# The first MoE's slices taken in halves: two pairs of batches in turn, with their sums in two parts through DRAM

## The chip, the cores and the metric

The kernel runs on one core of a Trainium2 chip. The core has a matrix engine (TensorE, PE in the profile), VectorE (DVE), ScalarE (ACT), GpSimd (POOL), and SyncE (SP), whose queue issues nearly all transfers between DRAM and the on-chip memory. Each engine runs its instructions in the order in which the program has them; between engines, semaphores order the work. The metric is the device time of one execution in microseconds (us).

## The reference, cut to what matters

Three layers stand one behind the other. Batches are 8, heads 8, positions 576, head width 64; `x` has 8 x 576 = 4608 rows of 512.

```python
p_packed = sm_attn(p, k, v)                 # 32 packed rows per head attend to 576 keys
out = sm_attn(q, p_packed, p_packed)        # 576 rows per head attend to the 32 packed rows
x = out.transpose(0, 2, 1, 3).reshape(4608, 512)
h = max(max(x @ w1, x @ w2), x @ w3)        # first MoE: 512 -> 768
x2 = h @ w_out                              # 768 -> 512
h = x2 @ w_in2                              # second MoE: 512 -> 2048, then a ratio of polynomials g(h)
return g(h) @ w_out2
```

The weights arrive as 64-bit floats. TensorE multiplies in a reduced 32-bit form, so each operand is split into a high and a low part and each product takes three matmuls.

## The kernel before

**Stages.** The work up to `x2` goes by four pairs of batches, `bp` = 0 to 3; the second MoE follows in blocks of 512 rows and is not touched. Instead of forming `x`, the kernel multiplies the softmax of the second attention (`a2`) with `m`, the product of the packed values and the weights (`m_stage`, two for each slice). `h` has 768 columns, in six slices `f` of 128. For a pair, the loop over `f` and the two batches calls `y_stage`; each has three steps `w`, one for each of `w1`, `w2`, `w3`: 12 matmuls into a `psy` bank, then a copy to `hm` on ACT (`w` = 0) or a maximum into `hm` on DVE (`L451`). Such a step is called a turn here: 36 make the y part of a pair. Behind it eight `x2_stage`s (two batches, four column blocks `m`) sum all six slices with `w_out`, 36 matmuls each; the sum is copied to a tile `hm` by ACT, for `m` = 3 by DVE (`L467`), and stored to `x2_scr` in DRAM.

**What runs between the turns.** After each turn the function `between` calls an `m_stage` for the next slice, one step of a script (`PACK` in the y part, `SECOND` in the x2 part) with the attention of the next pair, and, at some turns, `feed.step()`. The script's letters: `L`, `W`, `l` load keys, values and queries; `S`, `T`, `V`, `Z` are the first attention of one of four units; `s`, `g` the second attention.

**Weights.** A `feed.step()` finishes one piece of weights and starts the next. `decode` turns a piece of 64-bit floats into two parts: `L75`, `L76`, `L88`, `L90` on DVE, `L77` and others on ACT, `L85` and `L95` on POOL. The 30 pieces of the first MoE (24 of `w123`, four per slice, 384 columns; 6 of `w_out`, 512 columns) come before and during pair 0, one at every turn from its start until they are used up. A `w123` piece goes into a tile `wt`, is used by pair 0 from there and stored to `w_scr`; pairs 1 to 3 load it again (72 loads). The 32 pieces of the second MoE (512 columns) are fed during pairs 1 to 3, through the same four `wt` buffers, and stored to DRAM.

**Order.** The order of instructions on each engine is not the order of the code alone: a list scheduler with a timeline of its own places each instruction once its inputs are ready there, so work of a later `feed.step()` can stand ahead of its turn. On the chip that order is fixed.

Of the kernel before, what the change touches and what calls it, by code (L numbers as in the profile page):

```python
# [33 lines left out]
def attn_moe_moe2_kernel(  # L34
# [206 lines left out]
    NKT, NPT = 4, 3  # L241
# [11 lines left out]
    def s2_stage(u, qt, done):  # L253
# [25 lines left out]
        ah = a2p.tile([128, S], F32R, name=f"a2h{g}{b2}")  # L279
        al = a2p.tile([128, S], F32R, name=f"a2l{g}{b2}")  # L280
# [154 lines left out]
    hp_pool = bstack.enter_context(tc.tile_pool(name="hp_pool", bufs=1))  # L435

    def y_stage(b2, f, m, a2, between):
# [15 lines left out]
        hh = hp_pool.tile([128, S], F32R, name=f"hh{b2}{f}")  # L453
        hl = hp_pool.tile([128, S], F32R, name=f"hl{b2}{f}")
# [37 lines left out]
    for f in range(1, 6):  # L492
        pieces += [w_piece(f, hp) for hp in HPS] + wo[f + 2 : f + 3]
# [16 lines left out]
    feed2 = None  # L510

    y_steps = {1: range(1, 36, 4), 2: range(1, 36, 4), 3: range(1, 32, 4)}
    windows = (), (0, 2, 4, 6), (1, 3, 5)
    for bp in range(NBP):
        turn = itertools.count()
        if bp == 1:
            feed2 = Feed(wp, w2_pieces(), bufs=NRAW)
        a2, mt = ahead.a2, ahead.mt
        hs = [[None] * 6, [None] * 6]
        if bp + 1 < NBP:  # L520
            ahead = Ahead(bp + 1)
            for x in "L0 W0 L1 W1".split():
                ahead.do(x)
            pack = ahead.steps(PACK)
        else:
            pack = iter(())
        for f in range(6):
            if f < 5:
                nmt = m_tiles(f + 1)

            def between(bp=bp, f=f):
                t = next(turn)
                if f < 5 and t % 6 in (1, 3):
                    m_stage(bp, t % 6 // 2, nmt)
                if t >= 2:
                    next(pack, None)
                if bp == 0:
                    feed.step()
                elif t in y_steps[bp]:
                    feed2.step()  # L540
# [3 lines left out]
            for b2 in range(2):  # L544
                hs[b2][f] = y_stage(b2, f, mt[b2], a2[b2], between)
            mt = nmt
        if bp + 1 < NBP:
            assert not list(pack)
            gen = ahead.steps(SECOND)
            if bp == 0:  # L550
                assert not feed.raw and not feed.half
            for b2 in range(2):
                for m in range(4):
                    x2_stage(2 * bp + b2, m, hs[b2])
                    next(gen, None)
                    if 4 * b2 + m in windows[bp]:
                        feed2.step()
            next(gen, None)
            assert not ahead.soft
        else:  # L560
            assert not feed2.raw and not feed2.half
# [21 lines left out]
            for b2 in range(2):  # L583
                for m in range(4):
# [135 lines left out]
```

## Time and profile before

| what | value |
|---|---|
| median of 3 runs | 1429.55 us (1428.72 to 1430.9) |
| the profiled execution's own time | 1429.64 us |
| its span, first to last instruction | 1427.9 us (1.7 us lie around it) |
| busy: PE, DVE, ACT, POOL | 1337.6, 1093.5, 893.0, 351.1 us |
| mean granted TensorE clock | 0.973 of full speed |
| first matmul of the second MoE | about 630 us |

The change touches what lies before about 630 us. Busy shares over the whole span are means over stages with different limits, so the stages have to be read one by one; the rows of a stretch give the busy time of each engine in it, the granted clock (1.00 is 2.4 GHz, 0.50 is 1.2 GHz) and the load of the DMA engines.

### The profile page before, as it was taken

To read this page: it belongs to the slowest core of one execution; us is meant where nothing else is said; L and a number is where in the kernel's file an instruction comes from. 1 tells how busy PE (TensorE), PEld (TensorE's weight loads), DVE (VectorE), ACT (ScalarE), POOL (GpSimd) and SP (SyncE) were. 2 spreads that over 40 slices of the span, in tenths; PEclk is the share of its full clock that TensorE was granted. 3 is DMA by queue.
4 is the path that set the end of the run, shared out by engine and by line. 5 is a ranking of instruction groups with operands and counts; after the bars stand their busy time and mean duration, and the time that the engine had idled before them with its cause. 6 is when DMAs were issued, how large, how long until landed. Compare 5 with 4: busy or idle time off the path is not lost.

```text
span 1427.9 us, 21290 instructions
## 1 busy us (share of the span) xinstructions
PE 1337.6 (94%) x8016; PEld 1140.2 (80%) x8016; DVE 1093.5 (77%) x1712; ACT 893.0 (63%) x1523; POOL 351.1 (25%) x350
## 2 busy tenths in 40 slices
PE   5468899998999899999999999999999999999998
PEld 2257799887988799998888888888888888888886
DVE  5999854668475848339897888978888888888887
ACT  4577743655355536337686766868677686676765
POOL 4676632447444555300010100101001010000000
PEclk9598999999999999999999999999999999999999
DMA  9757662768556645583010100101001010010000
GB/s 290 224 188 220 221 232 78 245 209 297 173 174 228 240 165 192 180 293 154 1 59 1 56 4 7 53 1 60 1 8 52 1 52 1 11 42 0 31 1 30
DMA packets 76743, 159.72 MB, mean 112 GB/s; under 512 B 11104, under 2 KB 35680, under 8 KB 75872
## 3 DMA queue, kind: packets, MB, share of 16 engines
q1 hardware_dynamic: 76352, 157.84, 33.0%
q8 instruction: 63, 1.03, 0.3%
q10 hardware_dynamic: 288, 0.52, 0.1%
q14 instruction: 40, 0.33, 0.1%
HBM read 113.25 MB, written 45.09 MB: 111 GB/s over the span
## 4 chain that ended last, share of the span: by engine, by line
PE 76%; DMA 7%; DVE 3%; ACT 2%; issue 1%; SPq 0%; POOL 0%; DVEq 0%; ACTq 0%; POOLq 0%
PE po L61 9%; PE po L63 9%; PE po L62 9%; PE psh L62 9%; PE psh L61 9%; PE psh L63 9%; PE psy L61 6%; PE psy L63 6%; PE psy L62 6%; DMA w_raw<-in_w_dram 3%; DMA wi_b<-w_scr 2%; DMA w_scr<-wt 1%; DVE wt L88 1%; PE pst L363 1%; DVE ml L58 1%
## 5 line engine op out<-in xcount | busy, mean ns | idle before, releaser
L619 ACT ACTIVATE hb<-psh,babs 128x512 f32<-128x512 f32 (+1 forms) x145 | 100.1, 690 | 190.0 <-PE psh L63 190.0
L61 PE MATMUL po<-wq_b,gh 128*128 128x512 f32 x540 | 212.3, 393 | 0.8 <-ACT gh L54 0.8
L62 PE MATMUL po<-wq_b,gh 128*128 128x512 f32 x540 | 211.3, 391 | 0.0
L61 PE MATMUL psy<-a2h,mh 128*128 128x288 f32 x576 | 179.9, 312 | 31.3 <-ACT hm L449 13.8
L62 PE MATMUL psh<-xl,wi_b 128*128 128x512 f32 x504 | 196.9, 391 | 0.0
L63 PE MATMUL psh<-xh,wi_b 128*128 128x512 f32 x504 | 196.6, 390 | 0.0
L61 PE MATMUL psh<-xh,wi_b 128*128 128x512 f32 x504 | 196.5, 390 | 0.0
L58 POOL TENSOR_TENSOR xl<-xr,xh 128x512 fp32r<-128x512 f32 x28 | 36.5, 1304 | 627.7 <-ACT xh L54 627.7
L622 DVE SCALAR_TENSOR_TENSOR hb<-h,babs,hb 128x512 f32<-128x512 f32 (+1 forms) x145 | 108.3, 747 | 98.1 <-ACT h L620 98.0
L63 PE MATMUL po<-wq_b,gl 128*128 128x512 f32 x540 | 181.7, 391 | 0.0
L63 PE MATMUL psy<-a2h,ml 128*128 128x288 f32 x576 | 173.3, 301 | 2.5 <-DVE ml L58 2.4
L62 PE MATMUL psy<-a2l,mh 128*128 128x288 f32 x576 | 172.8, 300 | 0.0
L61 PEld LDWEIGHTS psy<-a2h,mh 128*128 128x128 f32 x576 | 110.9, 193 | 43.2 <-ACT hm L449 17.2
L61 PE MATMUL psy<-hh,wo_h 128*128 128x288 f32 x384 | 115.9, 302 | 9.6 <-ACT hm L467 8.6
L63 PEld LDWEIGHTS po<-wq_b,gl 128*128 128x128 f32 x540 | 101.3, 188 | 24.0
L61 PEld LDWEIGHTS po<-wq_b,gh 128*128 128x128 f32 x540 | 101.4, 188 | 22.9 <-ACT gh L54 1.2
L62 PEld LDWEIGHTS po<-wq_b,gh 128*128 128x128 f32 x540 | 101.4, 188 | 22.5
L451 DVE TENSOR_TENSOR hm<-psy,hm 128x576 f32<-128x576 f32 x96 | 72.4, 754 | 58.3 <-PE psy L63 54.6
L63 PE MATMUL psy<-hh,wo_l 128*128 128x288 f32 x384 | 115.0, 299 | 0.0
L62 PE MATMUL psy<-hl,wo_h 128*128 128x288 f32 x384 | 114.9, 299 | 0.0
L621 ACT ACTIVATE u<-psh,av 128x512 f32<-128x512 f32 (+1 forms) x145 | 113.9, 785 | 1.6 <-DVE gl L58 1.6
L627 DVE SCALAR_TENSOR_TENSOR u<-u,av,h 128x512 f32<-128x512 f32 (+1 forms) x145 | 107.8, 743 | 8.3 <-ACT h L624 8.3
(114 smaller groups left out, 3203.4 us busy)
## 6 DMA issues: line engine op xcount, KB each, us to landing
wt<-w_scr SPq DMA_DIRECT2D x72, 384.0 KB, 4.4
w_raw<-in_w_dram SPq DMA_DIRECT2D x32, 512.0 KB, 5.0
w_scr<-wt SPq DMA_DIRECT2D x32, 512.0 KB, 4.3
kt<-in_k_dram SPq DMA_DIRECT2D x16, 576.0 KB, 5.2
vraw<-in_v_dram SPq DMA_DIRECT2D x16, 576.0 KB, 6.7
w_raw<-in_w_dram SPq DMA_DIRECT2D x24, 384.0 KB, 3.4
kt<-in_q_dram SPq DMA_DIRECT2D x16, 576.0 KB, 6.7
w_scr<-wt SPq DMA_DIRECT2D x24, 384.0 KB, 3.4
```

The costliest lines, as they stand in the source:

```text
L58: e.tensor_tensor(out=lo, in0=src, in1=hi.bitcast(F32), op=ALU.subtract)
L61: pe.matmul(out_ap, lhsT=lh, rhs=rh, start=first, stop=False)
L62: pe.matmul(out_ap, lhsT=lh, rhs=rl, start=False, stop=False)
L63: pe.matmul(out_ap, lhsT=ll, rhs=rh, start=False, stop=last)
L88: dve.scalar_tensor_tensor(out=hib, in0=hw, scalar=-0x80000000, in1=t, op0=ALU.bitwise_and, op1=ALU.bitwise_or)
L363: pe.matmul(pv[32 * h : 32 * h + 32, :64], lhsT=at[:, 3 * i + cp, o : o + 32], rhs=vt[:, h, c, :], start=c == 0, stop=c == VC - 1)
L451: dve.tensor_tensor(out=hm, in0=ps[:, :, :288], in1=hm, op=ALU.max)
L619: act.activation(hb, h, AF.Abs, scale=babs[:, 0:1])
L621: act.activation(u, h, AF.Identity, scale=av[:, 3:4], bias=av[:, 2:3])
L622: dve.scalar_tensor_tensor(out=hb, in0=h2, scalar=babs[:, 1:2], in1=hb, op0=ALU.mult, op1=ALU.add)
L627: dve.scalar_tensor_tensor(out=u, in0=u, scalar=av[:, 0:1], in1=h2, op0=ALU.add, op1=ALU.mult)
```

## The change

The two first pairs take turns. A list `PHASES` replaces the loop over pairs: pair 0 with slices 0 to 2, pair 1 with slices 0 to 2, pair 0 with slices 3 to 5, pair 1 with slices 3 to 5, then pairs 2 and 3 with all six. They are called phase 0 to phase 5 here. The y part of phases 0 to 3 has 18 turns and their x2 part eight stages of 18 matmuls.

- In phases 0 and 1 `x2` is the sum over three slices, stored to `x2_scr` as before. In phases 2 and 3 `x2_load` fetches that partial sum into a tile `xs` (two buffers), and DVE adds the other three slices (`L486`), then it is stored again: 16 more stores, 16 loads and 16 DVE additions, while four DVE copies and twelve ACT copies that were there in pairs 0 and 1 stand now in phases 0 and 1.
- The pieces of slices 3 to 5 are needed from phase 2 on, and `FEED` says at which turns of each phase a `feed.step()` is called. Attention of pair 1 goes into phase 0, of pair 2 into phases 2 (first) and 3 (second), of pair 3 into phase 4.
- The pieces of slices 3 to 5 and all of the second MoE's are decoded into a tile `w2t` with one buffer. Only the 12 pieces of slices 0 to 2 are used where they were decoded; 84 loads of `wt` from `w_scr` take the place of 72.
- `wt` has 384 columns rather than 512, and keys and queries have three buffers (`NKT`) rather than four.

```diff
+    PHASES = (0, range(3)), (1, range(3)), (0, range(3, 6)), (1, range(3, 6)), (2, range(6)), (3, range(6))
+    ENTRIES = [(bp, f) for bp, fs in PHASES for f in fs]
...
     def w_piece(f, hp):
...
         def tiles():
-            box.append(wp.tile([128, 2, 512], F32R, name="wt", bufs=NWT)[:, :, :384])
-            wt_ready.append(box[0])
-            return box[0][:, 0, :], box[0][:, 1, :]
+            if f < 3:
+                box.append(wp.tile([128, 2, 384], F32R, name="wt", bufs=NWT))
+                wt_ready.append(box[0])
+                return box[0][:, 0], box[0][:, 1]
+            box.append(wp.tile([128, 2, 512], F32, name="w2t", bufs=1)[:, :, :384])
+            hi, lo = box[0][:, 0], box[0][:, 1]
+            return (hi.bitcast(I32) if wide else hi.bitcast(F32R)), lo.bitcast(F32R)
...
-        return wt, (n if NW <= n < NBP * NW else None)
+        return wt, (n if 3 * NHP <= n < NHP * len(ENTRIES) else None)
...
-            nc.sync.dma_start(wt.bitcast(F32), w_scr[n // NHP % 6, HPS[n % NHP]])
+            nc.sync.dma_start(wt.bitcast(F32), w_scr[ENTRIES[n // NHP][1], HPS[n % NHP]])
...
             def tiles(box=box):
-                box.append(wp.tile([128, 2, 512], F32R, name="wt", bufs=NWT).bitcast(F32))
+                box.append(wp.tile([128, 2, 512], F32, name="w2t", bufs=1))
...
-    NKT, NPT = 4, 3
+    NKT, NPT = 3, 3
...
+    def x2_load(b, m):
+
+        xs = kp.tile([128, 2, 288], F32, name="xs", bufs=2)
+        nc.sync.dma_start(xs.rearrange("p a b -> p (a b)"), x2_scr[:, m, S * b : S * b + S])
+        return xs
+
-    def x2_stage(b, m, hs):
+    def x2_stage(b, m, fs, hs, xs=None):
...
-        xs = hx.tile([128, 2, 288], F32, name="hm")
-        (act.copy if m < 3 else dve.tensor_copy)(xs, ps[:, :, :288])
+        if xs is None:
+            xs = hx.tile([128, 2, 288], F32, name="hm")
+            (act.copy if m < 3 else dve.tensor_copy)(xs, ps[:, :, :288])
+        else:
+            dve.tensor_tensor(out=xs, in0=ps[:, :, :288], in1=xs, op=ALU.add)
         nc.sync.dma_start(x2_scr[:, m, S * b : S * b + S], xs.rearrange("p a b -> p (a b)"))
...
+    FEED = [{*range(8), 10, 14, 18, 22}, {*range(0, 18, 2), 20}, {*range(1, 26, 5)}, {*range(1, 26, 4)},
+            {*range(1, 36, 3), 37, 39, 41, 43}, {*range(0, 24, 4)}]
...
+    for ph, (bp, fs) in enumerate(PHASES):
...
+        def tick():
+            t = next(turn)
+            next(script, None)
+            if t in FEED[ph]:
+                feed.step()
+            return t
...
+            for i, (b2, m) in enumerate(parts):
+                if ph in (2, 3) and i < 7:
+                    sums.append(x2_load(2 * bp + parts[i + 1][0], parts[i + 1][1]))
+                x2_stage(2 * bp + b2, m, fs, hs[b2], sums.pop(0) if sums else None)
+                tick()
```

How the order moves, at two places. First VectorE between the last turn of a y part and the next y part. Before, at the end of pair 0's x2 part (`sm`, `e` belong to the second attention of pair 1, `L467` is the last DVE copy of an `x2_stage`, `L451` the first maximum of pair 1):

```order
L274 RECIPROCAL sm_2313<-sm_2313 128x18 [waits DVE_49]
L272 TENSOR_REDUCE sm_2380<-e 128x18 [waits Activation_49]
L278 STREAM_TRANSPOSE hm<-e 128x576 [waits Pool_49]
L273 TENSOR_SCALAR sm_2380<-sm_2380 128x18 [waits DVE_49]
L274 RECIPROCAL sm_2380<-sm_2380 128x18 [waits DVE_49]
L278 STREAM_TRANSPOSE hm<-e 128x576 [waits Pool_49]
L467 COPY hm<-psy 128x576 [waits PE_49,Pool_49]
L451 TENSOR_TENSOR hm<-psy,hm 128x576 [waits DMAHW3_49,DMAHW4_49,DMAHW1_49,DMAHW5_49,PE_49,Activation_49]
L451 TENSOR_TENSOR hm<-psy,hm 128x576 [waits DVE_49,PE_49]
```

After the change, in phase 1's x2 part (`L484` the two copies, `L462` the first maximum of phase 2; `DMAHW` with a number is the semaphore of a transfer, one of eight that take turns):

```order
L484 COPY hm<-psy 128x576 [waits DMAHW5_49,PE_49,Activation_49]
L88 SCALAR_TENSOR_TENSOR w2t<-w_raw,dec_t 128x512 [waits DMAHW0_49,DVE_49]
L90 TENSOR_SCALAR dec_w<-w2t 128x512 [waits DVE_49]
L75 TENSOR_SCALAR dec_t<-w_raw 128x512 [waits DMAHW6_49]
L76 TENSOR_SCALAR dec_r<-w_raw 128x512 [waits Pool_49]
L88 SCALAR_TENSOR_TENSOR w2t<-w_raw,dec_t 128x512 [waits DMAHW4_49,DVE_49,Activation_49]
L90 TENSOR_SCALAR dec_w<-w2t 128x512 [waits DVE_49]
L75 TENSOR_SCALAR dec_t<-w_raw 128x512 [waits DMAHW3_49]
L484 COPY hm<-psy 128x576 [waits DMAHW1_49,DMAHW5_49,PE_49,Activation_49]
L76 TENSOR_SCALAR dec_r<-w_raw 128x512 [waits Pool_49]
L462 TENSOR_TENSOR hm<-psy,hm 128x576 [waits DMAHW6_49,DMAHW2_49,DMAHW7_49,PE_49,Activation_49]
```

The second attention has moved to phase 0, and pieces of the second MoE stand there in its place: each `L88` waits for the transfer that empties `w2t`, and the last copy and the first maximum stand behind such waits.

Second, SP's queue in an x2 part. Before, in pair 1's (`x_scr<-hm` the sums, `w_scr<-wt` decoded pieces of the second MoE, `w_raw` the next ones):

```order
L468 DMA x_scr<-hm 128x576 [waits DMAHW1_49,Activation_49]
L100 DMA w_raw<-in_w_dram 128x1024 [waits DMAHW2_49,DVE_49,Pool_49]
L234 DMA kt<-in_k_dram 128x1152 [waits DMAHW3_49,PE_49]
L217 DMA w_scr<-wt 256x1x512 [waits DMAHW4_49,Pool_49]
L100 DMA w_raw<-in_w_dram 128x1024 [waits DVE_49]
L217 DMA w_scr<-wt 256x1x512 [waits Pool_49]
L234 DMA kt<-in_k_dram 128x1152 [waits DMAHW7_49,PE_49]
L468 DMA x_scr<-hm 128x576 [waits DMAHW0_49,Activation_49]
L199 DMA wt<-w_scr 128x2x384 [waits DMAHW1_49,PE_49]
L199 DMA wt<-w_scr 128x2x384 [waits DMAHW2_49,PE_49]
L100 DMA w_raw<-in_w_dram 128x1024 [waits DMAHW3_49,DVE_49,Pool_49]
L217 DMA w_scr<-wt 256x1x512 [waits DMAHW4_49,Pool_49]
```

After, in phase 2's (`xs<-x_scr` the partial sums' loads, `x_scr<-xs` the stores of the full sums):

```order
L487 DMA x_scr<-xs 128x576 [waits DMAHW5_49,DVE_49]
L487 DMA x_scr<-xs 128x576 [waits DMAHW6_49,DVE_49]
L100 DMA w_raw<-in_w_dram 128x1024 [waits DMAHW7_49,DVE_49,Activation_49]
L472 DMA xs<-x_scr 128x576 [waits DMAHW5_49,DMAHW0_49]
L472 DMA xs<-x_scr 128x576 [waits DMAHW6_49,DMAHW1_49]
L227 DMA w_scr<-w2t 256x1x512 [waits DMAHW2_49,Pool_49]
L324 DMA vraw<-in_v_dram 96x1536 [waits DMAHW3_49,PE_49]
L487 DMA x_scr<-xs 128x576 [waits DMAHW4_49,DMAHW0_49,DVE_49]
L487 DMA x_scr<-xs 128x576 [waits DMAHW1_49,DVE_49]
L100 DMA w_raw<-in_w_dram 128x1024 [waits DVE_49,Activation_49]
L209 DMA wt<-w_scr 128x768 [waits DMAHW7_49,PE_49]
L209 DMA wt<-w_scr 128x768 [waits PE_49]
```

Each load of a partial sum now stands behind a store from the same buffer and waits for it, and stores and loads of two stages, one raw piece and one decoded piece follow each other in every group.

## Rows read from the trace of the kernel before

**Rows 1.** Busy time by stage: y and x2 part of pairs 0 to 3.

```profile
core 0: us, PE busy (x) PEld busy (x) DVE busy (x) ACT busy (x) POOL busy (x), PEclk, DMA share, GB/s
65.87:187.53 121.66, 97.32 (x788) 85.78 (x789) 104.31 (x169) 85.85 (x167) 78.82 (x83) 0.89 0.62 200
187.53:234.50 46.97, 46.62 (x372) 43.15 (x372) 24.58 (x41) 16.84 (x26) 19.07 (x15) 1.00 0.57 193
234.50:325.72 91.22, 84.63 (x772) 76.45 (x770) 58.36 (x97) 50.12 (x93) 40.34 (x48) 0.98 0.62 202
325.72:380.76 55.04, 49.66 (x370) 45.84 (x371) 38.17 (x62) 26.18 (x41) 36.05 (x26) 0.94 0.76 263
380.76:472.26 91.50, 84.77 (x773) 76.47 (x771) 60.33 (x98) 51.05 (x94) 40.27 (x48) 0.98 0.58 191
472.26:525.61 53.35, 49.47 (x379) 45.67 (x378) 35.93 (x57) 23.64 (x36) 32.42 (x24) 0.97 0.64 225
525.61:591.39 65.78, 64.35 (x470) 63.67 (x469) 45.72 (x60) 33.58 (x50) 29.88 (x21) 1.00 0.39 133
591.39:629.74 38.35, 38.35 (x290) 38.11 (x288) 5.34 (x8) 8.03 (x13) 1.43 (x1) 1.00 0.87 306
```

**Rows 2.** The same view, a shorter stretch inside pair 0's y part.

```profile
107.00:143.00 36.00, 29.02 (x275) 25.50 (x276) 32.63 (x59) 28.23 (x58) 24.25 (x28) 0.87 0.72 220
```

**Rows 3.** Groups on DVE, 234 to 591 us: busy us, mean ns | idle before.

```profile
L58 DVE TENSOR_TENSOR ml<-pst,mh 64x768 fp32r<-64x768 f32 x64 | 60.8, 953 | 13.8 <-ACT mh L54 12.7
L451 DVE TENSOR_TENSOR hm<-psy,hm 128x576 f32<-128x576 f32 x71 | 53.5, 754 | 49.2 <-PE psy L63 45.8 <-ACT hm L449 0.8 <-ACT dec_r L84 0.7
L88 DVE SCALAR_TENSOR_TENSOR wt<-w_raw,dec_t 128x512 int32<-128x512 int32 x31 | 29.8, 963 | 7.8 <-PE pst L63 4.1 <-DMA w_scr<-wt 3.6
L90 DVE TENSOR_SCALAR dec_w<-wt 128x512 int32<-128x512 int32 x31 | 20.4, 659 | 0.6
L76 DVE TENSOR_SCALAR dec_r<-w_raw 128x512 int32<-128x512 int32 x29 | 16.9, 582 | 1.6 <-POOL wt L95 1.6
L75 DVE TENSOR_SCALAR dec_t<-w_raw 128x512 int32<-128x512 int32 x29 | 15.5, 534 | 2.0 <-DMA w_raw<-in_w_dram 1.9
```

**Rows 4.** Transfers by kind: issuing queue, count, KB each, median us to landing.

```profile
wt<-w_scr SPq DMA_DIRECT2D x72, 384.0 KB, 4.4
w_raw<-in_w_dram SPq DMA_DIRECT2D x32, 512.0 KB, 5.0
w_scr<-wt SPq DMA_DIRECT2D x32, 512.0 KB, 4.3
kt<-in_q_dram SPq DMA_DIRECT2D x16, 576.0 KB, 6.7
x_scr<-hm SPq DMA_DIRECT2D x32, 288.0 KB, 2.4
xr<-x_scr SPq DMA_DIRECT2D x36, 256.0 KB, 2.8
```

**Rows 5.** All transfers from and to the weights' DRAM tile, 234 to 591 us.

```profile
DMA to landing us min/median/max: 3.1/4.4/9.1
```

**Rows 6.** Timeline from 258 us: one piece of the second MoE, and the next.

```profile
259.40 0.68 DVE L88 SCALAR_TENSOR_TENSOR wt<-w_raw,dec_t 128x512 int32<-128x512 int32 x1
...
261.59 1.30 POOL L95 TENSOR_TENSOR wt<-dec_r,dec_w 128x512 fp32r<-128x512 f32 x1 [0.50 <-PE psy L63]
...
262.91 0.58 SPq L217 DMA_DIRECT2D w_scr<-wt  x1
...
266.44 1.23 DVE L88 SCALAR_TENSOR_TENSOR wt<-w_raw,dec_t 128x512 int32<-128x512 int32 x1 [0.21 <-PE pst L63]
```

**Rows 7.** Timeline of PE in pair 1's x2 part, with the idle time ahead.

```profile
340.87 0.34 PE L63 MATMUL pst<-wt,pp 128*128 128x384 f32 x1
345.61 0.61 PE L61 MATMUL psy<-hh,wo_h 128*128 128x288 f32 x1 [4.40 <-ACT hm L467]
```

**Rows 8.** Busy time in shorter stretches of the x2 parts of pairs 1 and 3.

```profile
334.00:346.00 12.00, 7.60 (x60) 6.43 (x59) 9.13 (x15) 5.76 (x10) 5.74 (x5) 0.95 0.93 321
346.00:362.00 16.00, 16.00 (x113) 14.29 (x113) 14.78 (x26) 8.50 (x14) 13.80 (x10) 0.82 0.92 312
591.00:611.00 20.00, 20.00 (x153) 20.00 (x152) 1.45 (x2) 3.21 (x5) 1.43 (x1) 1.00 0.93 323
```

**Rows 9.** Who waited for the stores of `x2`, by the tile's view.

```profile
  ACT xh L54: 19.9, 7
  DVE hm L467: 7.2, 1
  ACT hm L467: 4.5, 2
```

More of the change, by code (lines that the diff above doesn't have):

```diff
@@ L432, in steps, with y_stage @@
                 yield
-    hp_pool = bstack.enter_context(tc.tile_pool(name="hp_pool", bufs=1))
-    def y_stage(b2, f, m, a2, between):
+    def y_stage(b2, place, m, a2, between):
         hm = hx.tile([128, 2, 288], F32, name="hm")
@@ L492, in attn_moe_moe2_kernel @@
     for f in range(1, 6):
-        pieces += [w_piece(f, hp) for hp in HPS] + wo[f + 2 : f + 3]
+        pieces += [w_piece(f, hp) for hp in HPS] + (wo[f : f + 1] if f > 2 else [])
     ahead = Ahead(0)
@@ L509, in attn_moe_moe2_kernel, with between @@
     pool.memset(cln[:, 1:2], -LN64)
[L510 to L540, printed above, removed]
+    a2s, k = {0: ahead.a2}, 0
+    mt = ahead.mt
+    aheads = {}
+    for ph, (bp, fs) in enumerate(PHASES):
+        turn, a2, size = itertools.count(), a2s[bp], 6 * len(fs)
+        hs = [[], []]
+        script = iter(())
+        if ph in AHEAD:
+            nb, text = AHEAD[ph]
+            if nb not in aheads:
+                aheads[nb] = ahead = Ahead(nb)
+                a2s[nb] = ahead.a2
+                for x in "L0 W0 L1 W1".split():
+                    ahead.do(x)
+            script = aheads[nb].steps(text)
+        if ph == 2:
+            assert not feed.raw and not feed.half
+            feed = Feed(wp, w2_pieces(), bufs=NRAW)
+        def tick():
[4 more added lines that the diff above has]
+            return t
+        for f in fs:
+            k += 1
+            now = k < len(ENTRIES) and (f != fs[-1] or ph not in (0, 4))
+            if now:
+                nmt = m_tiles(k)
+            def between():
+                t = tick() % 6
+                if now and t in (1, 3):
+                    m_stage(ENTRIES[k][0], t // 2, nmt)
             if bp == NBP - 1 and f == 2:
@@ L544, in attn_moe_moe2_kernel @@
             for b2 in range(2):
[L545 to L559, printed above, removed]
+                at = (3 * ph + f % 3) % 4 if ph < 4 else f
+                hs[b2].append(y_stage(b2, at, mt[b2], a2[b2], between))
+            mt = nmt if now else None
+        if bp < NBP - 1:
+            parts = [(b2, m) for b2 in range(2) for m in range(4)]
+            sums = [x2_load(2 * bp, 0)] if ph in (2, 3) else []
+            for i, (b2, m) in enumerate(parts):
[3 more added lines that the diff above has]
+                tick()
+            assert not list(script)
+            if mt is None:
+                mt = aheads[ENTRIES[k][0]].mt
+                assert not aheads[ENTRIES[k][0]].soft
         else:
-            assert not feed2.raw and not feed2.half
+            assert not feed.raw and not feed.half
             rstack.close()
```

50 lines of the change are left out of this document (33 added, 17 removed).

## The prediction

> **What bounds the kernel now.** I read the page's slices first, which show TensorE nearly full behind 630 us and not ahead of it, and then cut the time ahead of it into stages [rows 1]. Each pair has a y part (36 turns) and an x2 part (eight stages). Pair 3 has no attention beside it and shows what TensorE needs by itself: 65.78 us for 36 turns, 1.83 each, and 38.35 us for the x2 part, 4.79 a stage. What a next pair's attention adds is the difference to rows with it and with little else: 91.22 - 65.78 = 25.4 us in a y part (6.4 for each of four units), 46.97 - 38.35 = 8.6 us in an x2 part. So a pair with attention beside it should take 65.8 + 25.4 + 38.35 + 8.6 = 138.1 us. Pair 0 took 121.66 + 46.97 = 168.6, pair 1 91.22 + 55.04 = 146.3, pair 2 144.9.
>
> Pair 0's 30.5 us too many lie in its y part: VectorE is busy 104.31 of 121.66 us (86%), 32.63 of 36 us (91%) in the densest stretch [rows 2]; decoding sets the pace there, while the x2 part behind it uses VectorE 24.58 of 46.97 us. Pair 1's 8 us too many lie in its x2 part, where pieces of the second MoE are decoded and the DMA engines run at 263 GB/s. There ScalarE waited for a store of `x2` [rows 9], TensorE stood 4.40 us [rows 7], and the granted clock of the 16 us from there on was 0.82, that is, part of it ran at 1.2 GHz [rows 8].
>
> **The change, part by part.**
>
> *TensorE's own work.* The matmuls are the same, in other places. Phases 0 and 1 together hold 36 turns, eight stages' worth of `x2` and one pair's attention: 138.1 us bare. So do phases 2 and 3. Nothing is won here; the gain can only come from the excess, 30.5 + 8.2 us in the first two pairs, and 6.8 + 0 in the last two.
>
> *Phases 0 and 1, VectorE.* In the new order 24 pieces are decoded between the first maximum of phase 0 and the first of phase 2, against 20 in pair 0, and there are two more copies. A decoded piece costs VectorE 963 + 659 + 582 + 534 = 2.74 us, a copy or maximum 0.75 [rows 3]. Load: 104.31 + 24.58 + 4 x 2.74 + 1.5 = 141.4 us. It is spread better: only about 13.7 us of it (three pieces, two copies, three `ml` of 0.95) fall in phase 1's x2 part. The other 127.7 us lie beside 138.1 - 19.2 = 118.9 us of TensorE's, so VectorE remains the fuller engine. Bounds for its share are 86% (148 us) and 91% (140 us); I take 88%, 145 us.
>
> *The single `w2t`.* From `L88`'s start to the store's issue took 262.91 - 259.40 = 3.5 us [rows 6], the landing 4.3 in the median [rows 4], 3.1 to 9.1 [rows 5]. Until now this mattered little, since a piece took one of four `wt` buffers: VectorE idled 3.6 us for it in 31 pieces [rows 3], and the next `L88` came 7.04 us after the first [rows 6]. Now the next `L88` has to wait for the landing, so two can't stand closer than 3.5 + 4.3 = 7.8 us (6.6 to 12.6). VectorE takes its instructions in order, so maxima, copies, `ml` and additions stand behind the wait, and TensorE, with two `psy` banks, stops about two turns later. In a y part VectorE's other work fills about 7 us between two pieces, and the wait costs little. In the x2 parts it does not. Phase 1's: the last copy stands behind the third `L88` there; the piece before is issued about one turn ahead of the part: 3 x 7.8 - 1.8 + 0.96 + 0.75 = 23.3 us, against 19.2 bare. **Phases 0 and 1: 145 + 23.3 = 168 us, against 168.6; I put the gain at 1.**
>
> The Trainium skill, DMA: Bandwidth & Descriptors, "Anatomy of one DMA", gives a transfer about 2.0 us fixed and bytes over 436 GB/s, by my estimate 3.2 us for a piece's store. By that rule two `L88` could stand 6.7 us apart, under the 7.04 that VectorE needs anyway, and the sum would be the unchanged time of the third rival below. The row's median, 4.3 us, is 1.1 us above it on an engine with other transfers in its queue; I go by the row.
>
> *Phase 2.* Three units of attention in 18 turns: 32.9 + 3 x 6.4 = 52 us. Its x2 part has the rest, 19.2 + 6.4 = 25.6 us bare, but six pieces: the last two additions stand behind the fifth `L88`, whose first comes with the part's start: 4 x 7.8 + 0.96 + 1.5 = 33.7. The sixth stands ahead of phase 3's first maximum, 5 x 7.8 + 0.96 + 0.75 = 40.7, where TensorE would be at 33.7 + 2 x 1.83 = 37.4: 3.3 more, 37 us.
>
> *Phase 3.* VectorE has 12 maxima (9.0), nine `ml` (8.6), five pieces (13.7) and the second attention, which pair 0's x2 part puts at 24.58 - 8 x 0.95 - 1.5 - 2.7 = 12.8 us: 44 us, at 88% 50 us. TensorE bare: 32.9 + 8.6 = 41.5.
>
> *Phase 3's x2 part*, 19.2 us bare. Two paths run beside each other. Partial sums: no row shows a load into `xs`; the nearest is `xr` with 2.8 us, a store takes 2.4 [rows 4]. A buffer's round is store, load, addition: 2.4 + 2.8 + 0.75 plus the second of the two, about 6.7 us for two stages, which TensorE needs 4.8 for: 19.2 + 3 x 1.9 = 24.9. Bounds for a load are 0 (it is hidden) and 6.7 us (the slowest row, queries). Pieces: the last additions stand behind three intervals, 3 x 7.8 - 1.8 + 1.5 = 23.1, and a fourth `L88` ahead of the next maximum: 4 x 7.8 - 1.8 + 1.7 = 31.1, where TensorE would be at 26.8. With that 4.3: 27 us. The additions, 16 x 0.754 = 12.1 us, are inside these sums.
>
> **Phases 2 and 3: 52 + 37 + 50 + 27 = 166 us, against 146.3: 20 lost.**
>
> *Phases 4 and 5.* The scheduler has moved pieces forward: 7 against 12 in pair 2, none against 6 in pair 3. Phase 4's y part keeps 7, as before, and I leave it at 91.5. Its x2 part has none, like pair 0's with one: 47 instead of 53.35. Phase 5's y part can win at most what TensorE is idle, 65.78 - 64.35; I take 1. **Gain 7.**
>
> *At no cost:* twelve more `wt` loads (landing 4.4 us, issued four tiles ahead); three buffers for keys and queries instead of four (a load can come later by up to its landing, 6.7 us [rows 4], but VectorE sets the pace there); the ScalarE casts that the new tile saves, since ScalarE is less full than VectorE in all stages that the change touches [rows 1]. DMA: phases 2 and 3 move pair 1's 18.4 + 14.5 MB, and 24 transfers of 0.295 MB and 7 pieces of 1.05 MB more: 47 MB, 285 GB/s in 166 us. Rows reached 321 and 323 [rows 8], so it fits, but not with short landings.
>
> **Sum.** 1429.6 - 1 + 20 - 7 = 1441.6: **1442 us**. The profiled execution's time, 1429.64, is the median's within 0.1.
>
> **Rivals.**
> - *Levelling wins (faster).* If stores land in 3.1 us, `L88` needs 6.6 us and never waits, and VectorE keeps 91%: phases 0 and 1 take 140 + 20 = 160 (-8.6), phases 2 and 3 take 46 (half of pair 1's y part) + 32 + 48.5 + 25 = 151.5 (+5), phases 4 and 5 -7: 1419 us. For it speaks that VectorE was never held long by a store; against it, that this was with four buffers and less traffic. It decides below about 7 us between two `L88`.
> - *Landings get long (much slower).* At 285 GB/s transfers queue. With 6.5 us, halfway to the longest row, pieces stand 10 us apart: the three x2 parts cost 7 + 9 + 7 us more, the y parts of phases 2 and 3 some 10, and TensorE's gaps come with stretches at 1.2 GHz as in [rows 8]: 1475 us.
> - *No change.* Pieces at their shortest 6.6 us in the x2 parts, VectorE at 88%: phase 1's x2 part 20, phase 2's 31.5, phase 3's 25, which takes 11 us from my sum: 1431 us. The rule of the Trainium skill above comes out here.
>
> **How the numbers follow.** My forecast, some 1433 to 1455, gets 0.38; faster, mostly 1405 to 1426, 0.32; much slower 0.14; no change 0.16. What can be told from no change is about 0.2% (2.9 us). Slower is 0.38 + 0.14 = 0.52. The range from 1408 to 1462 leaves out about 0.1 on either side; the likeliest case alone spans 1433 to 1455.
>
> **What would show it.** In the profile after: VectorE's idle time ahead of `L88` in front of `w2t`, ended by the transfer from it, some 30 to 60 us over 44 pieces; x2 parts of phases 1, 2 and 3 near 23, 37 and 27 us; phases 0 and 1 together near 168 us with VectorE at 85% or more; pair 2's x2 part at 47. I am wrong if the waits for `w2t` are under 10 us in total, or if phases 0 and 1 fall under 155 us: then levelling wins.

## The result and the profile after

The changed kernel took 1445.86 us in the median of four runs (1443.11 to 1453.25), the kernel before 1429.13 us on the same chip (1428.01 to 1430.9). The ratio is 1.0124, 95% interval 1.0085 to 1.0163: slower by 1.2%. The profiled execution took 1445.43 us, its span is 1443.6.

The stages, cut as in [rows 1]: y and x2 part of phases 0 to 5 in turn (span of the stage first, then each engine's busy time and instructions, PE's clock, DMA share, GB/s).

```profile
60.01:130.42 70.41, 56.63 (x555) 46.33 (x556) 61.46 (x112) 46.99 (x98) 47.32 (x56) 0.89 0.72 233
130.42:162.90 32.48, 28.24 (x207) 25.16 (x207) 28.76 (x47) 20.61 (x35) 21.75 (x20) 1.00 0.92 317
162.90:208.13 45.23, 38.77 (x246) 37.12 (x247) 36.87 (x53) 28.64 (x46) 27.50 (x22) 0.92 0.74 247
208.13:230.19 22.06, 20.11 (x146) 19.14 (x145) 11.43 (x17) 12.56 (x19) 9.71 (x8) 1.00 0.65 228
230.19:279.75 49.56, 45.40 (x422) 40.31 (x420) 35.79 (x62) 28.81 (x55) 26.55 (x33) 0.97 0.76 251
279.75:322.90 43.15, 29.07 (x276) 26.99 (x272) 23.14 (x43) 18.73 (x34) 17.23 (x20) 0.90 0.95 333
322.90:373.96 51.06, 42.99 (x305) 38.30 (x305) 44.33 (x70) 28.71 (x44) 37.01 (x27) 0.90 0.72 244
373.96:404.56 30.60, 23.38 (x145) 22.45 (x144) 15.49 (x27) 11.40 (x17) 13.90 (x10) 0.86 0.70 243
404.56:495.84 91.28, 84.85 (x777) 77.89 (x777) 61.02 (x99) 50.66 (x92) 40.50 (x49) 0.98 0.64 214
495.84:543.42 47.58, 47.58 (x378) 44.17 (x377) 20.73 (x36) 12.73 (x19) 16.40 (x13) 1.00 0.36 129
543.42:606.99 63.57, 63.57 (x471) 63.57 (x470) 33.21 (x40) 27.04 (x39) 15.73 (x11) 1.00 0.19 64
```

Phases 0 and 1 take 170.2 us where pair 0 took 168.6 [rows 1]; phases 2 and 3 take 174.4 where pair 1 took 146.3; phase 4 takes 138.9 against 144.9, phase 5's y part 63.6 against 65.8, and the first turn comes at 60.0 instead of 65.9. So all that was lost but 1.6 us lies in phases 2 and 3 (28.1 us), most of it in their x2 parts, 43.15 and 30.60 us, in which TensorE is busy for 29.07 and 23.38.

Two waits stand out. First VectorE's at line 88 (idle us, times), in the view of that line:

```profile
  DMA w_scr<-w2t: 38.5, 28
```

Only 7.5 of these 38.5 us lie in the two long x2 parts; the same row of that view, cut to phase 2's and to phase 3's:

```profile
  DMA w_scr<-w2t: 6.4, 3
  DMA w_scr<-w2t: 1.1, 2
```

Second, in the view of the tile `xs`, VectorE's wait for a first partial sum, and TensorE's and its weight load's for the addition:

```profile
  DMA xs<-x_scr: 8.7, 7
...
  PEld psy L61: 21.6, 8
  PE psy L61: 19.7, 7
```

The chain of waits on the profile's page names the first: it is the only transfer there with such a share of the span.

```profile
PE po L61 9%; PE po L62 9%; PE po L63 9%; PE psh L62 9%; PE psh L61 9%; PE psh L63 9%; DMA w_scr<-w2t 8%; PE psy L61 5%; PE psy L63 4%; PE psy L62 4%; POOL w2t L95 2%; DMA w_raw<-in_w_dram 1%; DVE w2t L88 1%; DVE ml L58 1%; DVE dec_w L90 1%
```

The longest gap of TensorE in these parts, at the end of phase 2's, shows how the two lie together. Three engines' rows of the timeline, SP, VectorE and TensorE apart (start, duration, instruction, idle time before it and what ended it):

```profile
309.15 0.32 SPq L487 DMA_DIRECT2D x_scr<-xs  x1
...
311.65 0.32 SPq L487 DMA_DIRECT2D x_scr<-xs  x1
313.47 0.52 SPq L227 DMA_DIRECT2D w_scr<-w2t  x1
314.95 1.17 SPq L209 DMA_DIRECT2D wt<-w_scr  x2
316.21 1.36 SPq L472 DMA_DIRECT2D xs<-x_scr  x2
```

```profile
308.36 0.76 DVE L486 TENSOR_TENSOR xs<-psy,xs 128x576 f32<-128x576 f32 x1 [0.53 <-DMA xs<-x_scr]
...
310.87 0.76 DVE L486 TENSOR_TENSOR xs<-psy,xs 128x576 f32<-128x576 f32 x1
...
313.47 0.43 DVE L76 TENSOR_SCALAR dec_r<-w_raw 128x512 int32<-128x512 int32 x1 [1.18 <-POOL w2t L95]
318.57 0.69 DVE L88 SCALAR_TENSOR_TENSOR w2t<-w_raw,dec_t 128x512 int32<-128x512 int32 x1 [4.67 <-DMA w_scr<-w2t]
...
322.09 1.51 DVE L486 TENSOR_TENSOR xs<-psy,xs 128x576 f32<-128x576 f32 x2 [0.45 <-DMA xs<-x_scr]
```

```profile
315.12 0.34 PE L63 MATMUL pst<-wt,pp 128*128 128x384 f32 x1
322.90 0.61 PE L61 MATMUL psy<-hh,mh 128*128 128x288 f32 x1 [7.45 <-DVE xs L486]
```

TensorE stands 7.45 us for two additions. Ahead of them VectorE stood 4.67 us at line 88, which looks like the cause. But the first buffer went round like this, with the landing times from the trace: addition at 308.36, its store issued at 309.15 and landed 5.9 us later at 315.0, the next load into the buffer issued at 316.21 and landed 5.8 us later at 322.0, the next addition at 322.09. VectorE, once through with its piece, still waited 0.45 us for that load. Without the wait at line 88 the additions could have come earlier by some 0.1 us. The round took 322.09 - 308.36 = 13.7 us here.

The twelve loads that follow a store from their buffer in these two parts all show this: each was issued at most 1.2 us after that store had landed, and eleven of the twelve additions started within 0.15 us of their load's landing (the other 0.5 us after it).

### The profile page after: what moved, and what is told of

The parts are those of the page before. It is cut to its first block, busy times and chain, and to the rows that moved or that the text cites. A ratio compares the mean times of both kernels' runs of the same rounds, so it can differ in the third digit from the quotient of the medians.

```text
span 1443.6 us, 21341 instructions
## 1 busy us (share of the span) xinstructions
PE 1342.0 (93%) x8016; PEld 1144.5 (79%) x8016; DVE 1094.3 (76%) x1728; ACT 891.7 (62%) x1511; POOL 348.2 (24%) x350
## 3 DMA queue, kind: packets, MB, share of 16 engines
q8 instruction: 63, 1.03, 0.3%
## 4 chain that ended last, share of the span: by engine, by line
PE 70%; DMA 12%; DVE 8%; POOL 3%; issue 3%; ACT 2%; SPq 0%; POOLq 0%; DVEq 0%; ACTq 0%
PE po L61 9%; PE po L62 9%; PE po L63 9%; PE psh L62 9%; PE psh L61 9%; PE psh L63 9%; DMA w_scr<-w2t 8%; PE psy L61 5%; PE psy L63 4%; PE psy L62 4%; POOL w2t L95 2%; DMA w_raw<-in_w_dram 1%; DVE w2t L88 1%; DVE ml L58 1%; DVE dec_w L90 1%
## 5 line engine op out<-in xcount | busy, mean ns | idle before, releaser
L61 PE MATMUL psy<-a2h,mh 128*128 128x288 f32 x432 | 134.6, 312 | 20.6 <-ACT mh L54 7.0
L63 PE MATMUL psy<-a2h,ml 128*128 128x288 f32 x432 | 130.4, 302 | 0.2 <-DVE ml L58 0.2
L62 PE MATMUL psy<-a2l,mh 128*128 128x288 f32 x432 | 130.3, 302 | 0.1
L61 PEld LDWEIGHTS psh<-xh,wi_b 128*128 128x128 f32 x504 | 94.6, 188 | 20.7
L62 PEld LDWEIGHTS psh<-xl,wi_b 128*128 128x128 f32 x504 | 94.7, 188 | 20.3
```

The costliest lines, as they stand in the source:

```text
L61: pe.matmul(out_ap, lhsT=lh, rhs=rh, start=first, stop=False)
L62: pe.matmul(out_ap, lhsT=lh, rhs=rl, start=False, stop=False)
L63: pe.matmul(out_ap, lhsT=ll, rhs=rh, start=False, stop=last)
```

## The experiments

Three theories were tried. **Chain** (the prediction's): a single `w2t` holds VectorE at line 88. **Round trip**: the partial sums' way through DRAM with two `xs` buffers. **Load**: decoding itself, wherever it is put. Each run is compared with the kernel before on the same chip; the chips were not all the same, so kernels are compared by their ratios. The stage columns come from one profiled execution of each kernel, which can lie some us off the median (e5's took 1427.6 us, e9's 1422.1). All runs in one table: the median, the ratio to the kernel before on the same chip with its interval, and from each profile phases 0 + 1, the x2 parts of phases 2 and 3 together, phase 4 (y and x2), and VectorE's idle time at line 88 until a transfer out of `w2t` (us).

| kernel | median us | ratio, 95% interval | ph. 0+1 | x2 of 2+3 | ph. 4 | at L88 |
|---|---|---|---|---|---|---|
| changed kernel | 1445.9 | 1.0124 (1.0085-1.0163) | 170.2 | 73.8 | 138.9 | 38.5 |
| e1 two w2t, two w_raw | 1465.2 | 1.0249 (1.0231-1.0266) | 191.0 | 76.2 | 131.4 | 1.5 |
| e2 two w_raw | 1458.6 | 1.0208 (1.0192-1.0223) | 181.5 | 70.0 | 142.4 | 20.1 |
| e3 no loads | 1428.4 | 1.0006 (0.9992-1.0019) | 168.4 | 49.4 | 145.4 | 38.0 |
| e4 before, one w2t | 1429.0 | 1.0005 (0.9990-1.0020) | | | | 30.8 |
| e5 eight loads ahead | 1423.6 | 0.9976 (0.9961-0.9992) | 169.8 | 45.1 | 148.0 | 30.6 |
| e6 e5 + two w2t | 1433.2 | 1.0040 (1.0025-1.0055) | 187.7 | 45.5 | 131.3 | 2.6 |
| e7 sum later | 1427.9 | 1.0002 (0.9985-1.0019) | 166.5 | 48.4 | 146.9 | 45.0 |
| e8 ScalarE's queue | 1451.5 | 1.0165 (1.0131-1.0200) | 171.1 | 75.7 | 142.8 | 30.2 |
| e9 e5 + late pieces | 1428.5 | 1.0002 (0.9986-1.0018) | 165.4 | 46.6 | 142.5 | 23.8 |
| e10 e5 + w2t, w2u | 1424.5 | 0.9980 (0.9966-0.9994) | 169.5 | 50.1 | 135.0 | 5.6 |
| e11 four xs | 1419.9 | 0.9944 (0.9927-0.9960) | 168.3 | 46.6 | 144.8 | 25.8 |
| e12 three xs | 1430.5 | 1.0018 (1.0005-1.0030) | 168.0 | 54.1 | 145.4 | 30.7 |

### e1 and e2: a second w2t, paid for with a w_raw

```diff
-    NRAW = 3
+    NRAW = 2
...
-  box.append(wp.tile([128, 2, 512], F32, name="w2t", bufs=1)...
+  box.append(wp.tile([128, 2, 512], F32, name="w2t", bufs=2)...
```

e2 has the first of the two edits alone.

> The changed kernel with two buffers for w2t in place of one; the 4 KB for it come from w_raw (two buffers in place of three). Chain theory (one w2t buffer holds VectorE at L88 until the store has landed): VectorE's idle time at L88 under a transfer falls from 38.5 us to under 10, the x2 stretches of phases 2 and 3 (43.2 + 30.6) fall by 10 to 18 together, total 1428 to 1436 if w_raw costs nothing. Load theory (the decode work itself in those phases is what costs): waits at L88 go, but the time does not, 1442 to 1449. Round-trip theory (the partial sums' way through DRAM is what costs): 1441 to 1447, the waits on L486 stay at 20 us.

> The changed kernel with two w_raw buffers in place of three and nothing else, so that the run with two w2t buffers can be read. All theories: within 3 us of 1446 if the third raw buffer is spare (a piece is loaded one step ahead, some 10 us, and lands in about 4); 1450 to 1460 if VectorE now waits for raw pieces.

With two `w2t` the wait at line 88 all but goes, 38.5 to 1.5 us, and the time rises by 1.2% (ratio 1.0249 against 1.0124), outside all three ranges on record for e1. The third `w_raw` is not spare: in e2, in the view of the tile, VectorE and ScalarE stand longer for raw pieces; the changed kernel has 30.0 us in 29 waits in the same row.

```profile
  DMA w_raw<-in_w_dram: 93.2, 46
```

That cost makes e1 hard to read by itself, but e1 against e2 says that taking 18.6 us of waits away at line 88 bought nothing. Chain did not expect that; e6 and e10 below ask it again with three `w_raw`.

e1 also shows the round trip by itself: all pieces are decoded before phase 3's x2 part there, the DMA engines are at 0.47, and the part takes 23.4 us:

```profile
404.70:428.09 23.39, 19.80 (x147) 19.11 (x145) 9.53 (x12) 3.54 (x5) 3.43 (x3) 1.00 0.47 152
```

### e3: the partial sums without their loads

```diff
         xs = kp.tile([128, 2, 288], F32, name="xs", bufs=2)
-        nc.sync.dma_start(xs..., x2_scr[:, m, S * b : S * b + S])
...
-            dve.tensor_tensor(out=xs, in0=ps[:, :, :288], in1=xs, op=ALU.add)
+            dve.tensor_copy(xs, ps[:, :, :288])
```

> The changed kernel without the loads of the 16 first partial sums in phases 2 and 3; VectorE copies the second partial sum instead of adding (the first half of the sum is left out of x2). Round-trip theory: the 8.7 us at L486 under a load go, and with them PE's 20 us behind L486, total 1424 to 1434. Chain theory: PE waited for L486 because VectorE stood at L88 before it; 1438 to 1446, L88's 38.5 us stay within 10. Traffic theory (14 MB more through the queues lengthen each store's landing): store landing falls from 4.5 to about 4.1 us, total 1440.

The kernel leaves out the first half of the sum in `x2`. The 17 us are gone, while VectorE's wait at line 88 stays at 38.0 us in all. The x2 parts of phases 2 and 3, and the wait:

```profile
278.97:307.69 28.72, 25.27 (x258) 24.11 (x255) 17.78 (x34) 12.61 (x24) 13.03 (x15) 0.94 0.85 283
359.92:380.60 20.68, 19.65 (x146) 19.42 (x146) 14.84 (x22) 9.19 (x14) 10.86 (x8) 0.98 0.70 239
```

```profile
  DMA w_scr<-w2t: 38.0, 23
```

So the loads, with the waits that hang on them, are what made the change slower. The same 44 pieces are decoded here, so load is not the main cause. Against chain the total says less than it seems: in the two x2 parts themselves the waits at line 88 come to 4.5 us, against 7.5 in the changed kernel. e7 below has more of them there.

### e4: the kernel before with a single w2t

```diff
-  box.append(wp.tile([128, 2, 512], F32R, name="wt", bufs=NWT).bitcast(F32))
+  box.append(wp.tile([128, 2, 512], F32, name="w2t", bufs=1))
```

and `wt` is 384 wide.

> The kernel before, with wt 384 wide and the 32 pieces of the second MoE decoded into a single w2t (as in the changed kernel, but in the old order, where two such pieces are 10 to 20 us apart). Chain theory: a single buffer costs only where pieces follow within about 8 us, so 1426 to 1433, and VectorE's wait at L88 under a transfer stays under 8 us. If one buffer costs wherever it is (rival): 32 pieces by 1 to 1.4 us as in the changed kernel, 1440 or more.

The time is unchanged, as chain expected, but not for its reason: the wait at line 88 is 30.8 us here too, not under 8, where [rows 3] had 3.6.

```profile
  DMA w_scr<-w2t: 30.8, 19
```

Even in the old order VectorE can stand for 31 us there without a net price. Its first turn comes at 65.61 us, so `wt`'s width is not what made the changed kernel's start shorter.

### e5: all eight loads ahead

```diff
     def x2_load(b, m):
-        xs = kp.tile([128, 2, 288], F32, name="xs", bufs=2)
+        x, g, b2 = "hl"[m % 2], m // 2, b % 2
+        if b < 2:
+            xs = a2p.tile([128, S], F32R, name=f"a2{x}{g}{b2}")
+        else:
+            xs = hp_pool.tile([128, S], F32R, name=f"h{x}{b2}{4 + g}")
...
+                if ph in (2, 3) and f == fs[-1]:
+                    sums += [x2_load(2 * bp + b2, m) for m in range(4)]
...
```

> The changed kernel with the first partial sums loaded into eight tiles that are free by then (the a2 tiles of the pair whose first MoE is just done), four as each batch ends, in place of two xs buffers; w2t stays single. A round trip through DRAM that has only two buffers as the cause (a load starts when the store of two stages earlier has landed: 3.1 + 4.5 + 0.8 us for two stages of 2.8 us of PE): the x2 stretches of phases 2 and 3 fall from 43.2 + 30.6 to about 50 together, 1422 to 1432. Traffic or VectorE's queue as the cause: 1438 to 1447. The chain theory of the prediction (single w2t): at most 5 us gained, 1440 to 1446.

Loads, additions and traffic are those of the changed kernel; only their buffers and times differ. The two x2 parts fall to 25.6 and 19.5 us and the kernel is faster than the one before. Traffic and VectorE's additions are out as causes. Phase 4's y part gave 9 us back in this execution: pieces that had lain in the long x2 parts are decoded there now (VectorE's order has line 88 14 times between the last maxima of phases 3 and 4; the changed kernel has it 11 times).

```profile
280.74:306.35 25.61, 23.60 (x258) 22.77 (x255) 14.34 (x28) 10.27 (x21) 9.85 (x13) 1.00 0.91 324
...
358.12:377.59 19.47, 19.31 (x146) 19.08 (x145) 14.72 (x23) 7.47 (x11) 9.50 (x7) 1.00 0.78 283
377.59:477.84 100.25, 87.37 (x778) 78.65 (x777) 68.59 (x117) 60.33 (x109) 53.85 (x59) 0.97 0.71 244
```

### e6 and e10: a second w2t without the cost of w_raw

```diff
 e6:  w2t with bufs=2, for slices 3 to 5 and for the second MoE
 e10: - box.append(wp.tile([128, 2, 512], F32, name="w2t", bufs=1))
      + box.append(wp.tile([128, 2, 512], F32, name=("w2t", "w2u")[i % 2], bufs=1))
```

Both are e5 with this edit; e10 leaves slices 3 to 5 on the single tile.

> The kernel with the loads ahead in eight tiles, and with the 4.6 KB that xs leaves free given to a second w2t (three w_raw stay). Chain theory: 5 to 15 us below the run with loads ahead alone. If waiting at L88 costs nothing because VectorE's work is not what comes last there: within 3 us of it; slower by 5 to 20 if, as with two w2t and two w_raw, pieces are put earlier into stretches whose VectorE is full.

> The kernel with the loads ahead; pieces of the second MoE go in turn to w2t and to a second tile of the same size, slices 3 to 5 stay on the single w2t. If the two w2t buffers cost 10 us because pieces are placed earlier, into phases 0 and 1, and not through the buffers themselves: phases 0 and 1 stay at 170 us as with loads ahead (in place of 188 with two w2t), total 1420 to 1428, VectorE's wait at L88 under a transfer falls below 10 us without a gain beyond 4 us. Chain theory: 1410 to 1418. If a second buffer costs wherever it is: 1430 or more.

e6 takes the wait from 30.6 to 2.6 us and loses 10 us; e10 takes it to 5.6 and ends within 1 us of e5 (the intervals overlap). In e6 VectorE's order has line 88 39 times up to the last maximum of phase 1, against 32 in e5 and 33 in e10. Pieces fall where VectorE is the fuller engine; x2 of phase 0, both parts of phase 1, y of phase 2:

```profile
129.53:173.72 44.19, 33.86 (x214) 30.52 (x214) 41.11 (x65) 27.34 (x47) 32.64 (x29) 0.88 0.90 304
173.72:227.83 54.11, 42.10 (x240) 39.08 (x240) 50.45 (x62) 34.15 (x54) 38.21 (x27) 0.84 0.76 271
227.83:249.65 21.82, 19.96 (x145) 19.19 (x145) 17.79 (x23) 14.16 (x24) 12.97 (x10) 1.00 0.82 280
249.65:307.07 57.42, 47.28 (x452) 41.77 (x452) 48.32 (x78) 37.96 (x70) 38.71 (x41) 0.94 0.92 320
```

VectorE is busy 93% of the first two, and phases 0 and 1 take 187.7 us, against 169.8 in e5 and 169.5 in e10. So e6's loss goes with the earlier order of the pieces; the single tile had held them back. What the wait at line 88 costs by itself can't be read from either run, since both move the order: e10's phases 2 and 3 take 9.2 us more than e5's and its phase 4 takes 13.0 less.

### e7: no loads, the sum made later

```diff
-            dve.tensor_tensor(out=xs, in0=ps[:, :, :288], in1=xs, op=ALU.add)
+        nc.sync.dma_start(dst[...], xs...)          # dst: x2_scr or x2b_scr
...
+    nc.sync.dma_start(xr2[:, :n], x2b_scr[:, kc, 512 * blk : 512 * blk + n])
+    pool.tensor_tensor(out=xr[:, :n], in0=xr[:, :n], in1=xr2[:, :n], op=ALU.add)
```

> The changed kernel with the second partial sums stored to a DRAM array of their own, and both added by GpSimd when the second MoE loads x2 (18 more loads of 256 KB or less there); no load in phases 2 and 3, copies as in phases 0 and 1. Round-trip theory: phases 2 and 3 as in the run without loads (some 150 us in place of 174), 1424 to 1432, if the adds stay hidden under PE in the second MoE; chain theory: 1440 to 1447.

As round trip expected: the x2 parts take 48.4 us together, with 45.0 us of waits at line 88, the longest of all runs. The time is that of the kernel before. And here the waits lie where chain wants them; cut to phase 2's and to phase 3's x2 part:

```profile
  DMA w_scr<-w2t: 6.6, 2
  DMA w_scr<-w2t: 7.7, 2
```

Those are 14.3 us, twice the changed kernel's, in parts that are 25 us shorter. That decides between chain and round trip.

### e8: the loads on ScalarE's queue

```diff
-        nc.sync.dma_start(xs..., x2_scr[:, m, S * b : S * b + S])
+        nc.scalar.dma_start(xs..., x2_scr[:, m, S * b : S * b + S])
```

> The changed kernel with the loads of the first partial sums issued by ScalarE in place of SP, still two xs buffers. If their place behind waiting entries of SP's queue is what makes them late: 1428 to 1435; if the two buffers are (a load waits for a store's landing wherever it is issued): 1441 to 1450, more if ScalarE stands at them.

No gain: the x2 parts stay at 75.7 us. The run by itself does not clear SP's queue, since the loads stand among ScalarE's own work now, and ScalarE stood 11.8 us in two waits for stores of `xs` ahead of line 77. But in the changed kernel the loads were issued 1.2 us or less after the landing that they had to wait for, so little could be won there.

### e9: pieces for phase 5

```diff
+                if ph < 5:
                     box.append(wp.tile([128, 2, 512], F32, name="w2t", bufs=1))
+                else:
+                    kt = kp.tile([128, 4 * 288], F32, name="kt", bufs=NKT)
+                    box.append(kt[:, :1024].rearrange("p (x n) -> p x n", x=2))
```

on top of e5, with the feeding turns of phases 3 to 5 spread later.

> The kernel with the loads ahead, and the pieces of the second MoE spread later: those fed in phase 5 are decoded into the kt buffers (three of 4.6 KB, free once the last attention is done, so that they can't be drawn forward), 9 of them where 2 lay there; phase 4 has 7 in place of 14. If VectorE's and GpSimd's work in phase 4 beside the last attention is what took back part of the gain (its y stretch is 100.2 us with loads ahead, 91.3 in the changed kernel): that stretch falls to 88 to 94, phase 5's y stretch stays under 66, total 1412 to 1419. If the place of the pieces makes no difference: 1421 to 1426. If phase 5 or the loads of the second MoE's weights suffer: above 1426.

Phase 4's y part fell as expected; what it won, its x2 part and phase 5 lost: 89.1 + 53.4 + 69.5 = 212.0 us against 211.5 in e5. In the ratios e9 is 0.26% slower than e5; these two executions, e9's 6.4 us below its median and e5's 4.0 above, don't show where.

```profile
371.62:460.68 89.06, 84.62 (x778) 78.17 (x777) 53.04 (x90) 49.54 (x90) 35.61 (x45) 0.98 0.58 196
460.68:514.08 53.40, 49.60 (x378) 45.58 (x376) 42.15 (x61) 21.69 (x35) 30.89 (x22) 0.97 0.59 216
514.08:583.61 69.53, 65.37 (x468) 65.14 (x469) 39.14 (x48) 30.12 (x44) 25.78 (x19) 0.98 0.27 94
```

The expectation of room in phase 5 failed. VectorE is busy 56% of that part and TensorE loses 6 us all the same; why was not followed up.

### e11 and e12: four and three buffers

```diff
...
-        xs = kp.tile([128, 2, 288], F32, name="xs", bufs=2)
+        n = next(loaded) % 4                       # e12: % 3
+        x, g = "hl"[n % 2], n // 2
+        if b < 2:
+            xs = a2p.tile([128, S], F32R, name=f"a2{x}{g}0")
+        else:
+            xs = hp_pool.tile([128, S], F32R, name=f"h{x}0{4 + g}")
```

> The changed kernel with four buffers for the first partial sums in place of two, each load still written one stage ahead. If the number of buffers is what made the round trip slow: x2 stretches of phases 2 and 3 together 45 to 58 us (73.7 with two, 45.1 with eight loads ahead), 1423 to 1432. If the loads have to be started ahead of the stretch: 60 or more, 1435 to 1444.

> The changed kernel with three buffers for the first partial sums (two: 73.7 us for the x2 stretches of phases 2 and 3; four: 46.5 us). By the cycle of one buffer, load 4.5 us + add 0.8 + store 3.1 = 8.4 us, three buffers allow a stage each 2.8 us, just what TensorE needs for one: 46 to 58 us, total 1420 to 1430. If four only helped by their place (tiles free earlier, no shared pool) and not by their number: also 46 to 50, so the same as four. If the cycle is longer than its three median parts (waits in SP's queue): 55 to 65, 1430 to 1438.

The x2 parts by the number of buffers: 73.8 us with two, 54.1 with three, 46.6 with four, 45.1 with eight. The cycle worked out from medians (8.4 us) gives 2.8 us a stage with three, 45 us in all; the 54.1 lie within the range on record and 9 us above that. With two it gives 16 x 4.2 = 67 us, 7 too few. The total of e12 is 0.5 us above its range, that of e11 3 below. e11's two x2 parts:

```profile
278.36:305.49 27.13, 25.10 (x259) 24.28 (x255) 15.45 (x28) 12.38 (x25) 10.66 (x14) 0.94 0.94 320
...
352.87:372.31 19.44, 19.35 (x146) 19.01 (x145) 14.62 (x23) 7.00 (x10) 10.14 (x8) 1.00 0.72 253
```

e11 is the best kernel of the study, 0.56% faster than before, with 25.8 us of waits at line 88. That three buffers end 10 us behind four, with 7.6 us in the x2 parts, and that four beat eight by some 4 us lies partly in the order of pieces, which differs; it was not taken apart.

## Why the prediction came out

The time (1442 forecast, 1445.9 measured) and the place were right, the main mechanism was not; that the number came out is luck.

**The single `w2t`: the step that failed.** The forecast put VectorE's idle time ahead of line 88 at 30 to 60 us, and it is 38.5. But "maxima, copies, `ml` and additions stand behind the wait, and TensorE, with two `psy` banks, stops" is what doesn't follow in the two x2 parts: only 7.5 of the 38.5 us lie there, and eleven of twelve additions started as soon as their load had landed. e3, e4, e7 and e11 have 26 to 45 us of the same waits and are no slower than the kernel before, and e6 and e10 take them away for no gain. A price of some 3 us is not excluded: the x2 parts take 48.4 us in e7, with 14.3 us of these waits, and 45.1 and 46.6 in e5 and e11, with 1. Phase 1's x2 part, forecast at 23.3 us and without such loads, took 22.1; with three `L88` in it, it takes 20.5 to 22.2 (also e3, e5, e8, e12), with two 19.0 to 19.6 (e7, e9, e11), but e6, with five and 1.3 us of waits, takes 21.8, so what of this is the wait stays open. The sums 4 x 7.8 and 3 x 7.8 in the x2 parts of phases 2 and 3 came near the measured lengths (37 and 27 forecast, 43.2 and 30.6 measured) by luck.

**Partial sums: mis-sized.** They had a path of their own in the forecast, 6.7 us for two stages, and only in phase 3, and it came out below the pieces' path. That is the path that sets the pace. Measured over the kernel, loads land in 4.5 us in the median and stores of `xs` in 3.1, where 2.8 and 2.4 were taken from [rows 4]:

```profile
xs<-x_scr SPq DMA_DIRECT2D x16, 288.0 KB, 4.5
x_scr<-xs SPq DMA_DIRECT2D x16, 288.0 KB, 3.1
```

With the addition that is 8.4 us, and 73.8 / 8 = 9.2 us as measured. The two parts differ; stores of line 487, then loads of line 472, first in phase 2's x2 part, then in phase 3's:

```profile
DMA to landing us min/median/max: 2.7/5.5/6.8
DMA to landing us min/median/max: 3.8/5.2/5.9
DMA to landing us min/median/max: 2.1/2.3/6.0
DMA to landing us min/median/max: 3.1/4.1/6.1
```

With 0.76 us for the addition these medians make a round of 11.5 us in phase 2 and 7.2 in phase 3; a part holds four, and 43.15 / 4 = 10.8 and 30.60 / 4 = 7.7 were measured. In e1's phase 3 stores took 2.1 and loads 3.0 us: a round of 5.9, and 23.39 / 4 = 5.8. So the forecast's 6.7 us was enough where little else moves. The DMA engines were at 0.95 in the first of these parts, 0.70 in the second and 0.47 in e1's, and the landings go with that; no run varied this load alone. The forecast had landings grow only in its rival, and there for the pieces. So the 20 us that were to be lost came as 28, by another path.

**Where the time sits.** Against e11, which keeps loads, additions and the single `w2t`: e11 runs phases 2 and 3 in 142.6 us, the changed kernel in 174.4. TensorE runs nearly the same number of matmuls in them (1150 and 1148), for 132.5 and 140.8 us, and idles 10.1 and 33.5. So of the difference of 31.8 us, 23.4 are idle time and 8.3 longer matmuls: the granted clock of the two x2 parts is 0.90 and 0.86 after gaps such as the 7.45 us one, that is, part of them ran at 1.2 GHz; in e11 it is 0.94 and 1.00.

**Phases 0 and 1** were forecast at 168 us and took 170.2; VectorE's load came out near the 141.4 us worked out, 138.5 us busy, but that is 81% of the time, not the 85% or more that was to show it. (The 13.7 us put into phase 1's x2 part are added up wrongly: three pieces, two copies and three `ml` make 12.6.) Levelling won little or nothing there in any run: 165 to 171 us in e3 and e5 to e12, e6 apart. **Phases 4 and 5** were to gain 7: phase 4 gained 6.0 and phase 5's y part 2.2. A part of the 6 is only lent: with short x2 parts ahead (e5, e11) phase 4 is back at 145 to 148. **The start**, 5.9 us shorter, was not in the sum; e4 excludes the width of `wt`, and the rest stays open.

**The rivals.** Levelling wins, 1419 us, is where e11 comes out, but by another way: `L88` waits 25.8 us there, and phases 0 and 1 take 168.3 us, not 160. The rule of the Trainium skill, DMA: Bandwidth & Descriptors, "Anatomy of one DMA — SWDGE (gpsimd) path", gives 3.2 us for a piece's store by my estimate; the section has it for transfers that GpSimd issues, and SP issued these. The median was 4.5 us in the changed kernel and 3.8 to 5.3 out of `w2t` in the experiments, so the rows decide; only e9's nine stores out of `kt` came near the rule, with 3.0 us.

## What to carry to other kernels

A wait that is as long as forecast is no proof of its price: take it away, or find a run that keeps it and is fast. Where partial results go through DRAM in a loop, count buffers by the whole round (load, use, store, all with their landings in loaded queues) over the time of a stage, and look for tiles that are free at that moment to hold them. A landing time taken from one stretch holds for the load of that stretch; take it again where more is moved. A second buffer in front of an in-order engine lets its work be placed earlier, and e6 shows that this can cost time where that engine is the fuller one.

## What was not expected of the hardware

The same decoding instruction of VectorE takes from 0.36 to 1.58 us with 384 columns, and 0.40 to 1.52 with 512; line 90 in the changed kernel, both widths together (min/median/max in ns):

```profile
L90 DVE TENSOR_SCALAR dec_w<-w2t x44: 359/427/1580, 96.3 to 464.8; 128x512 int32<-128x512 int32 x32, 128x384 int32<-128x384 int32 x12
```

Counted in the trace's records from 60 us on, those 35 beside which no GpSimd instruction ran took 0.43 us in the median, the 17 with GpSimd busy for over half of their time 1.0 (with 512 columns alone 26 of 0.43 and 7 of 1.03). In e6, where pieces are packed closer, 53 instructions of line 75 took 39.2 us in place of 28.5. So decoding took longer where it was packed closer: a piece's price by a mean, as in [rows 3], belongs to the density at which it was read. The Trainium skill, SBUF — State Buffer, "Who interferes with whom", says that VectorE in some modes and GpSimd share one pair of ports, which one holds for a whole instruction; the durations agree with that, but no run here moved GpSimd's work away to show it.
